# A decode attention kernel whose first V unit is split over two regions, with another layout for the transposed probabilities

## The chip, the cores and the metric

The kernel runs on one core of a Trainium2 chip. The metric is the device time of one execution in microseconds; the median of three runs before is 347.29 us.

## The reference

One decode step mixes two blocks with a gate. Attention has 2 batches, 32 heads, 4096 cached rows of 128, so K and V are 2 x 32 x 4096 x 128 bf16 each, 64 MB each: nearly all the data of the kernel.

```python
g = sigmoid((x * gate_w).sum(-1))                      # x: 2 x 1 x 512
q = (x @ wq) as (b, h, 1, 128)                         # 32 heads
p = softmax(einsum("bhqd,bhkd->bhqk", q, k_cache) * 128 ** -0.5)
a = einsum("bhqk,bhkd->bhqd", p, v_cache) as (b, 1, 4096) @ wo
b = maximum(x @ w1, 0) @ w2                            # 512 -> 1376 -> 512
out = g * a + (1 - g) * b
```

## The kernel before

**Units, halves and regions.** K and V are each cut into 8 units of 8 MB, unit u holding the rows of eight heads of one batch; each unit is laid over 128 partitions with 64 KB a partition. A half (`lo` or `hi`) is 4 MB. The buffer `kv` has five halves: region A (two), B (two), C (one). A piece is a unit in A or B, or a half in C (or in the first half of A or B). The lists `k_pieces` and `v_pieces` give the order by hand; `pieces` is K's ten, then V's ten. All pieces go out on SP's queue in that order (L279), and each waits for the marker `predecessor`: the last instruction that read the piece which held the same region (`holder`). Wait and issue are in order, so a piece that waits holds up all later ones. wq lies in C and w1 in B before K gets there; wo comes to C, and w2 to the upper half of B, after V.

**K.** Each half of a unit is four turns: VectorE transposes 128 x 2048 words in 32 x 32 blocks into one of three buffers `kt` (L393), and TensorE multiplies them with q (L400, L421), all scores staying in PSUM. The last transpose of a piece is its marker `k_read_n`.

**Softmax.** After the 64th turn VectorE takes the maximum (L429) and turns it about; ScalarE takes the four exponentials into `E_sb` (L441), laid out as [r, s] with 32 columns s for each r; VectorE transposes the 32 x 32 blocks in two instructions (L445) to `ET_sb`. `ET_sb` is [w, r]: for a fixed r, the 32 values of w that one block yields lie 64 elements (128 bytes) apart.

**V.** For each piece n, VectorE spreads the probabilities over a mask of eight groups (`v_spread`, L467) into `ptm`, one instruction for a piece (two for the first): 1024 elements a partition for a half, 2048 for a unit. Its source is read with neighbouring c 32 or 64 elements apart. TensorE multiplies them with the rows of V (`v_unit`, L482), 32 matmuls for a half and 64 for a unit, and the last is the marker `v_read_n`. VectorE takes the diagonal from PSUM (`v_extract`, L490, L493) into `X2`, five pieces to each batch. `v_spread` is called two pieces ahead, so on VectorE the spread of piece n + 2 stands in front of the extraction of piece n.

**End.** `o_gather` (L508 on) adds a batch's five pieces with f32 matmuls, scales them and turns them into `oW`; `project` (L527) multiplies by wo; `ffn_f` (L534) by w2 and adds; the output is stored.

Of the kernel before, what the change touches and what calls it, by code (L numbers as in the profile page):

```python
# [4 lines left out]
ALU = mybir.AluOpType  # L5
# [7 lines left out]

NKT = 3
HALF = 16384
REGION = {"A": 0, "B": 2 * HALF, "C": 4 * HALF}
WO_CUT = 24


# [68 lines left out]
def bass_gated_mix__gqa_block_cached__dense_activation_relu__decode_kernel(  # L88
# [39 lines left out]
    qbuf = sb("qbuf", [128, 4, 2, 4, 160], dt.bfloat16)  # L128
    kt_late = kt[:, :, :].rearrange("p k n -> p (k n)").bitcast(dt.bfloat16)
    E_sb = kt_late[:, 0:2048].rearrange("p (r s) -> p r s", s=32)  # L130
    ET_sb = kt_late[:, 2048:4096].rearrange("p (w r) -> p w r", r=64)
    ptm = kt_late[:, 4096:12288]
    q_late = qbuf[:].rearrange("p u a j m -> p (u a j m)").bitcast(dt.float32)
    X2 = q_late[:, 0:1280].rearrange("p (b k d) -> p b k d", b=2, d=128)
    pr_sb = q_late[:, 1280:1792]
    mpad = sb("mpad", [128, 32], dt.float32)
    mrow = sb("mrow", [128, 32], dt.float32)
    mmax = sb("mmax", [128, 8], dt.float32)
# [40 lines left out]
        P.sems[e] = nc.alloc_semaphore(e + "_ev")  # L179
    names = ["x", "gw", "wq", "w1", "wo0", "wo1", "w2a", "w2b", "w2c", "w2d", "out", "fin"]  # L180
    sem = {n: nc.alloc_semaphore("sem_" + n) for n in names}
    sem_region = {r: nc.alloc_semaphore("sem_region" + r) for r in "ABC"}

    mk = {}

    def marker(name):
        m = mk.get(name)
        if m is None:
            m = _Marker()
            mk[name] = m  # L190
        return m
# [2 lines left out]
    both, lo, hi = (0, 1), (0,), (1,)  # L194
    k_pieces = [(0, both, "A"), (1, both, "B"), (2, lo, "C"), (3, both, "A"), (4, both, "B"), (2, hi, "C"),
                (5, both, "A"), (6, both, "B"), (7, lo, "C"), (7, hi, "A")]
    v_pieces = [(0, both, "B"), (1, lo, "C"), (2, both, "A"), (3, both, "B"), (1, hi, "C"), (4, both, "A"),
                (5, both, "B"), (6, lo, "C"), (7, both, "A"), (6, hi, "B")]
    pieces = [("k", n, *p) for n, p in enumerate(k_pieces)] + [("v", n, *p) for n, p in enumerate(v_pieces)]
    landed, predecessor = {}, {}  # L200
    holder, filled = {"A": None, "B": "pe_h", "C": "pe_q"}, {"A": 0, "B": 0, "C": 0}
    for kind, n, u, halves, region in pieces:
        predecessor[kind, n] = holder[region]
        filled[region] += 1
        landed[kind, n] = (sem_region[region], 16 * filled[region])
        holder[region] = f"{kind}_read_{n}"

    turns = [(n, u, half, a, h, j == 0 and a == 0 and h == 0)
             for n, (u, halves, region) in enumerate(k_pieces) for j, half in enumerate(halves) for a in range(2) for h in range(2)]
# [60 lines left out]
    def sp(fn, waits=(), dwaits=()):  # L270
        P.add("sp", fn, waits=waits, dwaits=dwaits)
# [5 lines left out]
    for kind, n, u, halves, region in pieces:  # L277
        sp(lambda e, kind=kind, u=u, halves=halves, region=region:
           e.dma_start(piece_sb(halves, region), piece_in(kind, u, halves)).then_inc(sem_region[region], 16),  # L279
           waits=([marker(predecessor[kind, n])] if predecessor[kind, n] else []))  # L280
    sp(lambda e: e.dma_start(w2[0:96, 10, :], B_w2[1280:1376, :]).then_inc(sem["w2a"], 16), waits=[marker("v_read_6")])
    sp(lambda e: e.dma_start(wreg[:, 0:512 * WO_CUT], wo_in[:, 0:512 * WO_CUT]).then_inc(sem["wo0"], 16), waits=[marker("v_read_7")])
    sp(lambda e: e.dma_start(wreg[:, 512 * WO_CUT:HALF], wo_in[:, 512 * WO_CUT:HALF]).then_inc(sem["wo1"], 16))
    for name, r0, r1 in (("w2b", 0, 4), ("w2c", 4, 9), ("w2d", 9, 10)):
        sp(lambda e, name=name, r0=r0, r1=r1: e.dma_start(w2[:, r0:r1, :], w2a_in[:, r0:r1, :]).then_inc(sem[name], 16))
# [142 lines left out]
    def softmax():  # L428
        dve(lambda v: v.tensor_reduce(out=mpad[:, 0:2], in_=psf(0, 128, 0, 4 * BANK).rearrange("p (par n) -> p par n", par=2),  # L429
                                      axis=AX.X, op=ALU.max),  # L430
            waits=["pe_sc_63", "c_mpad"], signal="dve_m")
        dve(lambda v: v.transpose(out=mrow[:, :], in_=mpad[:, :]), waits=["dve_m"], signal="dve_mt")
        dve(lambda v: v.tensor_reduce(out=mmax[:], in_=mrow[:, :].rearrange("p (u c) -> p u c", c=4), axis=AX.X, op=ALU.max),
            waits=["dve_mt"], signal="dve_mm")
        dve(lambda v: v.tensor_scalar(out=nrow[:], in0=mmax[:].unsqueeze(2).to_broadcast([128, 8, 4]), scalar1=-INV_SQRT_DH,
                                      scalar2=None, op0=ALU.mult), waits=["dve_mm"], signal="dve_mn")
        dve(lambda v: v.transpose(out=negm[:, :], in_=nrow[:].rearrange("p u c -> p (u c)")),  # L437
            waits=["dve_mn"], signal="dve_neg")
        for g in range(2):
            for par in range(2):  # L440
                act(lambda a, g=g, par=par: a.activation(  # L441
                    out=E_sb[:, 32 * g:32 * g + 32, 16 * par:16 * par + 16], in_=psf(0, 128, (2 * par + g) * BANK, 512).rearrange("p (r s) -> p r s", s=16), func=ACT.Exp,
                    bias=negm[:, par:par + 1], scale=INV_SQRT_DH, accum_out=lsum[:, par, g:g + 1]),
                    waits=["dve_neg"], signal=f"act_exp{2 * g + par}")
            dve(lambda v, g=g: v.transpose(out=ET_sb[:, :, 32 * g:32 * g + 32].rearrange("p w r -> p r w"), in_=E_sb[:, 32 * g:32 * g + 32, :]),  # L445
                waits=[f"act_exp{2 * g + 1}"], signal=f"dve_et{g}")
        v_spread(0, 0, 32)
        v_spread(0, 32, 64)
        dve(lambda v: v.tensor_reduce(out=lrow[:], in_=lsum[:], axis=AX.X, op=ALU.add), waits=["act_exp3"], signal="dve_lrow")

    v_at, at = [], 0
# [5 lines left out]
        nh = len(v_pieces[n][1])  # L457
        return ptm[:, 1024 * v_at[n]:1024 * (v_at[n] + nh)].rearrange("p (n h c) -> p n h c", h=8, c=4)

    def v_spread(n, n0, n1):  # L460
        u, halves, region = v_pieces[n]
        nh = len(halves)
        w0 = 4 * u + 2 * halves[0]
        src = ET_sb[:, w0:w0 + 2 * nh, :].rearrange("p w r -> p (w r)").rearrange("p (c n) -> p n c", c=4)[:, n0:n1]
        used = {(v_at[n] + j) % 8 for j in range(nh)}
        prev = [m for m in range(n) if used & {v_at[m] + j for j in range(len(v_pieces[m][1]))}]
        dve(lambda v: v.tensor_tensor(out=v_weights(n)[:, n0:n1], in0=src.unsqueeze(2).to_broadcast([128, n1 - n0, 8, 4]),  # L467
                                      in1=mask8[:].unsqueeze(1).unsqueeze(3).to_broadcast([128, n1 - n0, 8, 4]), op=ALU.mult),
            waits=["dve_et1", "c_mask8"] + [f"v_read_{m}" for m in prev], signal=f"pt{n}_{n0}")

    def v_unit(n):
        u, halves, region = v_pieces[n]
        nn = 32 * len(halves)
        rows = piece_sb(halves, region).rearrange("p (c n d) -> p c n d", c=4, d=128)
        for j in range(nn):
            t = j % 4
            waits = []
            if j == 0:
                waits = [f"pt{n}_0"] + ([f"dve_m{n - 2}"] if n >= 2 else [])
            if n == 0 and j == 32:  # L480
                waits = ["pt0_32"]
            pe(lambda e, j=j, t=t: e.matmul(  # L482
                psf(32 * t, 32 * t + 32, V_BS[n % 2] * BANK, 512), lhsT=v_weights(n)[:, j],
                rhs=rows[:, :, j, :], start=(j < 4), stop=(j >= nn - 4), tile_position=(0, 32 * t)),
               waits=waits, dwaits=([landed["v", n]] if j == 0 else []), signal=(f"v_read_{n}" if j == nn - 1 else None))

    def v_extract(n):
        b, k = divmod(n, 5)
        parts = pr_sb.rearrange("p (c d) -> p c d", c=4)
        dve(lambda e: e.tensor_tensor(out=parts, in0=psf(0, 128, V_BS[n % 2] * BANK, 512).rearrange("p (c d) -> p c d", c=4),  # L490
                                      in1=maskc[:].unsqueeze(2).to_broadcast([128, 4, 128]), op=ALU.mult),
            waits=[f"v_read_{n}", "dve_maskc"] + ([f"dve_x{n - 1}"] if n else []), signal=f"dve_m{n}")
        dve(lambda e: e.tensor_reduce(out=X2[:, b, k, :], in_=parts.rearrange("p c d -> p d c"), axis=AX.X, op=ALU.add),  # L493
            waits=[f"dve_m{n}"], signal=f"dve_x{n}")
# [8 lines left out]
                signal=("dve_rinv" if b else None))  # L503

    def o_gather(b):
        for k in range(5):
            w0 = 24 - 8 * (v_pieces[5 * b + k][0] - 4 * b)
            pe(lambda e, k=k, w0=w0: e.matmul(psf(0, 32, O_C0, 128), lhsT=selx[:, w0:w0 + 32], rhs=X2[:, b, k, :],  # L508
                                              start=(k == 0), stop=(k == 4)),
               waits=[f"dve_x{5 * b + k}"] + (["dve_rinv", "dve_selx"] if k == 0 else []),  # L510
               signal=(f"pe_O{b}" if k == 4 else None))
        dve(lambda v, b=b: v.tensor_scalar(out=O_sb[:, b, :], in0=psf(0, 32, O_C0, 128), scalar1=rinv[:, b:b + 1],
                                           scalar2=gb[0:32, b:b + 1], op0=ALU.mult, op1=ALU.mult),
            waits=[f"pe_O{b}", "dve_rinv", "dve_g"], signal=f"dve_O{b}")
# [51 lines left out]
            k_scores(i - 1)  # L566
    k_scores(63)
    softmax()
    v_spread(1, 0, 32)
    for n in range(10):  # L570
        if n + 2 < 10:
            v_spread(n + 2, 0, 32 * len(v_pieces[n + 2][1]))
        v_unit(n)
        if n == 1:
            o_denominators()
        v_extract(n)
        if n == 5:
            o_gather(0)
    o_gather(1)
    project()  # L580
# [34 lines left out]
```

## Time and profile before

| | us |
|---|---|
| median of three runs | 347.29 (347.23 to 347.6) |
| the profiled execution's own time | 346.8 |
| its span, from first to last instruction | 345.3 |
| VectorE busy | 206.9 (60%) |
| TensorE busy | 198.2 (57%) |
| ScalarE busy | 14.8 (4%) |
| HBM read | 145.43 MB, 421 GB/s over the span |

Times in the profile count from the span's start. PE is TensorE's matmuls, PEld its weight loads, DVE VectorE, ACT ScalarE, SP the engine that issues the big transfers; L445 is line 445 of the kernel before. A group's row gives its count, then busy time and mean duration in ns, then the idle time ahead of it and what ended that. The chain that ended last is followed back from the last instruction. A transfer's time to landing counts from its issue, so it holds the time that it stood behind earlier ones.

### The profile page before, as it was taken

What the parts mean: (1) busy time and instruction counts of PE and PEld (TensorE: products, weight loads), DVE (VectorE), ACT (ScalarE), POOL (GpSimd) and SP (SyncE); (2) the same over time, 40 slices, a digit from 0 to 9 for tenths busy, and PEclk for the clock granted to TensorE, in tenths of its full rate; (3) what the DMA queues carried; (4) which work ended last, traced back from release to release, by engine and by line L of the source; (5) the groups of instructions that cost most, each with busy time, mean ns of one, the idle gap of its engine ahead of it and who ended that gap; (6) DMA issues with size and microseconds to landing.
All of it is one profiled execution on the core that took longest, in us unless ns stands there. A gap on an engine that the chain in (4) does not pass through costs nothing.

```text
span 345.3 us, 2491 instructions
## 1 busy us (share of the span) xinstructions
PE 198.2 (57%) x1230; PEld 54.0 (16%) x974; DVE 206.9 (60%) x129; ACT 14.8 (4%) x54; POOL 7.7 (2%) x20
## 2 busy tenths in 40 slices
PE   0430497997897996979999008150540523610655
PEld 0230021111111111211111003020210211200231
DVE  0400797996998996989998799741360060410131
ACT  1040001010001001000000300000000000000000
POOL 8000000000000000000000000000000000000000
PEclk9965599999899998998999757665785585665787
DMA  8998999989899999989989898999989899998995
GB/s 331 440 486 366 478 433 406 482 387 478 374 417 425 478 464 402 457 380 425 440 364 486 362 482 372 478 412 421 490 387 471 380 465 395 450 478 387 416 385 229
DMA packets 4019, 145.57 MB, mean 422 GB/s; under 512 B 453, under 2 KB 682, under 8 KB 938
## 3 DMA queue, kind: packets, MB, share of 16 engines
q1 hardware_dynamic: 4004, 145.43, 98.1%
q8 instruction: 8, 0.13, 0.1%
q14 instruction: 1, 0.01, 0.0%
q10 hardware_dynamic: 6, 0.00, 0.0%
HBM read 145.43 MB, written 0.00 MB: 421 GB/s over the span
## 4 chain that ended last, share of the span: by engine, by line
DMA 66%; DVE 19%; PE 13%; ACT 1%; issue 1%; SPq 0%; DVEq 0%
DMA kv<-in_A_k_cache_dram 28%; DMA kv<-in_A_v_cache_dram 24%; DVE kt L393 15%; DMA kv<-in_B_w_dram 11%; PE PS L482 4%; DMA kv<-in_A_wq_dram 4%; PE PS L421 3%; PE PS L400 3%; DVE kt L445 3%; PE PS L334 1%; PE PS L373 1%; DVE mpad L429 1%; DVE kt L467 1%; ACT qrow L347 0%; ACT kt L441 0%
## 5 line engine op out<-in xcount | busy, mean ns | idle before, releaser
L393 DVE STREAM_TRANSPOSE kt<-kv 128x2048 f32<-128x2048 f32 x64 | 141.1, 2273 | 24.5 <-DMA kv<-in_A_k_cache_dram 24.5
L421 PE MATMUL PS<-kt,qbuf 128*128 128x512 bf16 x256 | 106.3, 415 | 33.7 <-DVE kt L393 28.8
L400 PE MATMUL PS<-kt,qbuf 128*128 128x512 bf16 x256 | 105.7, 413 | 0.0
L482 PE MATMUL PS<-kv,kt 128*32 128x512 bf16 x512 | 46.9, 544 | 92.7 <-DMA kv<-in_A_v_cache_dram 76.7
L490 DVE TENSOR_TENSOR qbuf<-PS,maskc 128x512 f32<-128x512 f32 x10 | 6.9, 689 | 83.1 <-PE PS L482 83.0
L421 PEld LDWEIGHTS PS<-kt,qbuf 128*128 128x128 bf16 x256 | 25.6, 100 | 142.1 <-DVE kt L393 72.2
L482 PEld LDWEIGHTS PS<-kv,kt 128*32 128x32 bf16 x512 | 18.3, 129 | 120.3 <-issue 77.3
L467 DVE TENSOR_TENSOR kt<-kt,mask 128x1024 bf16<-128x1024 bf16 (+1 forms) x11 | 29.1, 2664 | 0.0
L329 ACT ACTIVATE qbuf<-PS 32x4 bf16<-32x4 bf16 (+1 forms) x40 | 7.6, 189 | 108.3 <-PE PS L400 106.9
L493 DVE TENSOR_REDUCE qbuf<-qbuf 128x128 f32<-128x512 f32 x10 | 10.2, 1019 | 0.3
L445 DVE STREAM_TRANSPOSE kt<-kt 128x1024 bf16<-128x1024 bf16 x2 | 9.3, 4825 | 1.5 <-ACT kt L441 1.5
L556 ACT ACTIVATE out_sb<-PS 2x128 bf16<-2x128 f32 x2 | 0.5, 270 | 146.9 <-PE PS L534 146.9
L334 PE MATMUL PS<-kv,xTw 128*32 128x512 bf16 x32 | 3.6, 631 | 3.2 <-DMA kv<-in_A_wq_dram 3.2
L441 ACT ACTIVATE kt<-PS,negm 128x512 bf16<-128x512 f32 x4 | 2.7, 684 | 58.8 <-DVE negm L437 58.8
L296 DVE COPY xT<-PS 128x12 bf16<-128x12 bf16 x1 | 0.2, 169 | 8.3 <-PE PS L293 8.3
L293 PE MATMUL PS<-ident,x_sb 3*128 3x3 bf16 x4 | 0.3, 166 | 8.0 <-DMA x_sb<-in_gate_w_dram 8.0
L350 DVE CAST qrow<-PS 128x256 bf16<-128x256 f32 x2 | 2.4, 1388 | 3.9 <-PE PS L334 3.9
L527 PE MATMUL PS<-kv,oW 128*2 128x512 bf16 x32 | 3.5, 618 | 1.8 <-DMA kv<-in_A_wo_dram 1.8
L232 POOL MEMSET qbuf<- 128x5120 bf16 x1 | 4.4, 4358 | 0.0
L508 PE MATMUL PS<-qbuf,selx 128*32 128x128 f32 x20 | 3.4, 325 | 0.3 <-DVE qbuf L493 0.3
L429 DVE TENSOR_REDUCE mpad<-PS 128x2 f32<-128x2048 f32 x1 | 2.3, 2292 | 2.2 <-PE PS L400 2.2
L530 DVE COPY qbuf<-PS 128x512 f32<-128x512 f32 x1 | 0.7, 692 | 4.5 <-PE PS L527 4.5
(62 smaller groups left out, 31.8 us busy)
## 6 DMA issues: line engine op xcount, KB each, us to landing
kv<-in_A_k_cache_dram SPq DMA_DIRECT2D x4, 4096.0 KB, 31.6
kv<-in_A_v_cache_dram SPq DMA_DIRECT2D x4, 4096.0 KB, 35.1
kv<-in_A_wq_dram SPq DMA_DIRECT2D x1, 4096.0 KB, 12.2
kv<-in_A_wo_dram SPq DMA_DIRECT2D x1, 3072.0 KB, 33.7
kv<-in_B_w_dram SPq DMA_DIRECT2D x1, 1376.0 KB, 15.0
kv<-in_A_wo_dram SPq DMA_DIRECT2D x1, 1024.0 KB, 35.8
kv<-in_B_w_dram SPq DMA_DIRECT2D x1, 640.0 KB, 37.7
kv<-in_B_w_dram SPq DMA_DIRECT2D x1, 512.0 KB, 36.6
```

What stands on the lines that cost most here:

```text
L232: pool(lambda g: g.memset(qbuf[:], 0.0), signal="c_qbuf")
L329: act(lambda a: a.activation(out=out, in_=src, func=ACT.Copy), waits=waits, signal=f"q_{b}_{u}_{blk}_{par}")
L334: pe(lambda e, n=n, t=t: e.matmul(psf(32 * (n % 4), 32 * (n % 4) + 32, (QR_B + n // 4) * BANK, 512), lhsT=xTw[:, t, :], rhs=wreg[:, t * 40 ...
L393: dve(lambda v: v.transpose(out=dst, in_=pairs[:, h, 64 * a:64 * a + 64, :]), waits=([f"pe_sc_{i - NKT}"] if i >= NKT else []), dwaits=([l ...
L400: return e.add_instruction(mybir.InstMatmult(start_tensor_calc=start, stop_tensor_calc=stop, tile_size=(128, 128), tile_position=(0, 0), l ...
L421: return e.matmul(out, lhsT=lhsT, rhs=rhs, start=start, stop=stop)
L429: dve(lambda v: v.tensor_reduce(out=mpad[:, 0:2], in_=psf(0, 128, 0, 4 * BANK).rearrange("p (par n) -> p par n", par=2), axis=AX.X, op=ALU ...
L445: dve(lambda v, g=g: v.transpose(out=ET_sb[:, :, 32 * g:32 * g + 32].rearrange("p w r -> p r w"), in_=E_sb[:, 32 * g:32 * g + 32, :]), wai ...
L467: dve(lambda v: v.tensor_tensor(out=v_weights(n)[:, n0:n1], in0=src.unsqueeze(2).to_broadcast([128, n1 - n0, 8, 4]), in1=mask8[:].unsqueez ...
L482: pe(lambda e, j=j, t=t: e.matmul(psf(32 * t, 32 * t + 32, V_BS[n % 2] * BANK, 512), lhsT=v_weights(n)[:, j], rhs=rows[:, :, j, :], start= ...
L490: dve(lambda e: e.tensor_tensor(out=parts, in0=psf(0, 128, V_BS[n % 2] * BANK, 512).rearrange("p (c d) -> p c d", c=4), in1=maskc[:].unsqu ...
L493: dve(lambda e: e.tensor_reduce(out=X2[:, b, k, :], in_=parts.rearrange("p c d -> p d c"), axis=AX.X, op=ALU.add), waits=[f"dve_m{n}"], si ...
```

## The change

Region A may now also be held as two halves, A and Ah. The V pieces become eleven: unit 0 as a half in Ah and a half in C, then the others, and unit 7 as two halves at the end, in A and Ah; unit 4 takes the place of unit 6 as the one that goes through C in halves. The first batch has five pieces, the second six. A piece waits for all the markers of what it overwrites. w2 and wo wait for the pieces that now hold B and C last.

`ET_sb` becomes [r, w]: the rows of a transposed block lie side by side, and each of the two transposes writes 1024 consecutive elements. The spread then reads neighbouring w: a unit is one instruction as before; a half is two instructions of 512 elements, one for each r2, each writing two of every four columns. The first spread is no longer cut into two by rows.

```diff
-REGION = {"A": 0, "B": 2 * HALF, "C": 4 * HALF}
+REGION = {"A": 0, "Ah": HALF, "B": 2 * HALF, "C": 4 * HALF}
...
-    ET_sb = kt_late[:, 2048:4096].rearrange("p (w r) -> p w r", r=64)
+    ET_sb = kt_late[:, 2048:4096].rearrange("p (r w) -> p r w", w=32)
...
-    v_pieces = [(0, both, "B"), (1, lo, "C"), (2, both, "A"), (3, both, "B"), (1, hi, "C"), (4, both, "A"),
-                (5, both, "B"), (6, lo, "C"), (7, both, "A"), (6, hi, "B")]
+    v_pieces = [(0, lo, "Ah"), (1, both, "B"), (0, hi, "C"), (2, both, "A"), (3, both, "B"), (4, lo, "C"), (5, both, "A"),
+                (6, both, "B"), (4, hi, "C"), (7, lo, "A"), (7, hi, "Ah")]
+    n_first = 5
...
     for kind, n, u, halves, region in pieces:
-        predecessor[kind, n] = holder[region]
+        parts = ["A", "Ah"] if region == "A" and len(halves) == 2 else [region]
+        predecessor[kind, n] = [m for r in parts for m in holder[r]]
...
-           waits=([marker(predecessor[kind, n])] if predecessor[kind, n] else []))
-    sp(lambda e: e.dma_start(w2[0:96, 10, :], B_w2[1280:1376, :]).then_inc(sem["w2a"], 16), waits=[marker("v_read_6")])
-    sp(lambda e: e.dma_start(wreg[:, 0:512 * WO_CUT], wo_in[:, 0:512 * WO_CUT]).then_inc(sem["wo0"], 16), waits=[marker("v_read_7")])
+           waits=[marker(m) for m in predecessor[kind, n]])
+    sp(lambda e: e.dma_start(w2[0:96, 10, :], B_w2[1280:1376, :]).then_inc(sem["w2a"], 16), waits=[marker(holder["B"][0])])
+    sp(lambda e: e.dma_start(wreg[:, 0:512 * WO_CUT], wo_in[:, 0:512 * WO_CUT]).then_inc(sem["wo0"], 16), waits=[marker(holder["C"][0])])
...
-            dve(lambda v, g=g: v.transpose(out=ET_sb[:, :, 32 * g:32 * g + 32].rearrange("p w r -> p r w"), in_=E_sb[:, 32 * g:32 * g + 32, :]),
+            dve(lambda v, g=g: v.transpose(out=kt_late[:, 2048 + 1024 * g:3072 + 1024 * g].rearrange("p (r w) -> p r w", w=32), in_=E_sb[:, 32 * g:32 * g + 32, :]),
                 waits=[f"act_exp{2 * g + 1}"], signal=f"dve_et{g}")
-        v_spread(0, 0, 32)
-        v_spread(0, 32, 64)
+        v_spread(0)
...
+        def spread(out, src, nc_, **kw):
+            shape = [128, src.shape[1], 8, nc_]
+            dve(lambda v: v.tensor_tensor(out=out, in0=src.unsqueeze(2).to_broadcast(shape),
+                                          in1=mask8[:].unsqueeze(1).unsqueeze(3).to_broadcast(shape), op=ALU.mult), waits=waits, **kw)
+
+        if len(halves) == 2:
+            spread(v_weights(n), ET_sb[:, :, w0:w0 + 4], 4, signal=f"pt{n}")
+        else:
+            for r2 in range(2):
+                spread(v_weights(n)[:, :, :, r2:4:2], ET_sb[:, 32 * r2:32 * r2 + 32, w0:w0 + 2], 2, signal=(f"pt{n}" if r2 else None))
...
     def o_gather(b):
-        for k in range(5):
+        mine = range(n_first) if b == 0 else range(n_first, len(v_pieces))
+        for n in mine:
```

More of the change, by code (lines that the diff above doesn't have):

```diff
@@ L130, in bass_gated_mix__gqa_block_cached__dense_activation_relu__decode_kernel @@
     E_sb = kt_late[:, 0:2048].rearrange("p (r s) -> p r s", s=32)
-    ET_sb = kt_late[:, 2048:4096].rearrange("p (w r) -> p w r", r=64)
+    ET_sb = kt_late[:, 2048:4096].rearrange("p (r w) -> p r w", w=32)
     ptm = kt_late[:, 4096:12288]
     q_late = qbuf[:].rearrange("p u a j m -> p (u a j m)").bitcast(dt.float32)
-    X2 = q_late[:, 0:1280].rearrange("p (b k d) -> p b k d", b=2, d=128)
-    pr_sb = q_late[:, 1280:1792]
+    X2 = q_late[:, 0:1536].rearrange("p (b k d) -> p b k d", b=2, d=128)
+    pr_sb = q_late[:, 1536:2048]
     mpad = sb("mpad", [128, 32], dt.float32)
@@ L181, in bass_gated_mix__gqa_block_cached__dense_activation_relu__decode_kernel @@
     sem = {n: nc.alloc_semaphore("sem_" + n) for n in names}
-    sem_region = {r: nc.alloc_semaphore("sem_region" + r) for r in "ABC"}
+    sem_region = {r: nc.alloc_semaphore("sem_region" + r) for r in REGION}
     mk = {}
@@ L196, in bass_gated_mix__gqa_block_cached__dense_activation_relu__decode_kernel @@
                 (5, both, "A"), (6, both, "B"), (7, lo, "C"), (7, hi, "A")]
-    v_pieces = [(0, both, "B"), (1, lo, "C"), (2, both, "A"), (3, both, "B"), (1, hi, "C"), (4, both, "A"),
-                (5, both, "B"), (6, lo, "C"), (7, both, "A"), (6, hi, "B")]
+    v_pieces = [(0, lo, "Ah"), (1, both, "B"), (0, hi, "C"), (2, both, "A"), (3, both, "B"), (4, lo, "C"), (5, both, "A"),
+                (6, both, "B"), (4, hi, "C"), (7, lo, "A"), (7, hi, "Ah")]
+    n_first = 5
     pieces = [("k", n, *p) for n, p in enumerate(k_pieces)] + [("v", n, *p) for n, p in enumerate(v_pieces)]
     landed, predecessor = {}, {}
-    holder, filled = {"A": None, "B": "pe_h", "C": "pe_q"}, {"A": 0, "B": 0, "C": 0}
+    holder = {"A": [], "Ah": [], "B": ["pe_h"], "C": ["pe_q"]}
+    filled = {r: 0 for r in REGION}
     for kind, n, u, halves, region in pieces:
-        predecessor[kind, n] = holder[region]
+        parts = ["A", "Ah"] if region == "A" and len(halves) == 2 else [region]
+        predecessor[kind, n] = [m for r in parts for m in holder[r]]
         filled[region] += 1
         landed[kind, n] = (sem_region[region], 16 * filled[region])
-        holder[region] = f"{kind}_read_{n}"
+        for r in parts:
+            holder[r] = [f"{kind}_read_{n}"]
     turns = [(n, u, half, a, h, j == 0 and a == 0 and h == 0)
@@ L458, in v_weights, with v_spread @@
         return ptm[:, 1024 * v_at[n]:1024 * (v_at[n] + nh)].rearrange("p (n h c) -> p n h c", h=8, c=4)
-    def v_spread(n, n0, n1):
+    def v_spread(n):
         u, halves, region = v_pieces[n]
-        nh = len(halves)
         w0 = 4 * u + 2 * halves[0]
-        src = ET_sb[:, w0:w0 + 2 * nh, :].rearrange("p w r -> p (w r)").rearrange("p (c n) -> p n c", c=4)[:, n0:n1]
-        used = {(v_at[n] + j) % 8 for j in range(nh)}
+        used = {(v_at[n] + j) % 8 for j in range(len(halves))}
         prev = [m for m in range(n) if used & {v_at[m] + j for j in range(len(v_pieces[m][1]))}]
-        dve(lambda v: v.tensor_tensor(out=v_weights(n)[:, n0:n1], in0=src.unsqueeze(2).to_broadcast([128, n1 - n0, 8, 4]),
-                                      in1=mask8[:].unsqueeze(1).unsqueeze(3).to_broadcast([128, n1 - n0, 8, 4]), op=ALU.mult),
-            waits=["dve_et1", "c_mask8"] + [f"v_read_{m}" for m in prev], signal=f"pt{n}_{n0}")
+        waits = ["dve_et1", "c_mask8"] + [f"v_read_{m}" for m in prev]
+        def spread(out, src, nc_, **kw):
[7 more added lines that the diff above has]
+                spread(v_weights(n)[:, :, :, r2:4:2], ET_sb[:, 32 * r2:32 * r2 + 32, w0:w0 + 2], 2, signal=(f"pt{n}" if r2 else None))
     def v_unit(n):
@@ L478, in v_unit @@
             if j == 0:
-                waits = [f"pt{n}_0"] + ([f"dve_m{n - 2}"] if n >= 2 else [])
-            if n == 0 and j == 32:
-                waits = ["pt0_32"]
+                waits = [f"pt{n}"] + ([f"dve_m{n - 2}"] if n >= 2 else [])
             pe(lambda e, j=j, t=t: e.matmul(
@@ L487, in v_extract @@
     def v_extract(n):
-        b, k = divmod(n, 5)
+        b, k = divmod(n, n_first) if n < n_first else (1, n - n_first)
         parts = pr_sb.rearrange("p (c d) -> p c d", c=4)
@@ L505, in o_gather @@
     def o_gather(b):
-        for k in range(5):
[L507 to L511, printed above, removed]
+        mine = range(n_first) if b == 0 else range(n_first, len(v_pieces))
+        for n in mine:
+            w0 = 24 - 8 * (v_pieces[n][0] - 4 * b)
+            pe(lambda e, n=n, w0=w0: e.matmul(psf(0, 32, O_C0, 128), lhsT=selx[:, w0:w0 + 32], rhs=X2[:, b, n - mine[0], :],
+                                              start=(n == mine[0]), stop=(n == mine[-1])),
+               waits=[f"dve_x{n}"] + (["dve_rinv", "dve_selx"] if n == mine[0] else []),
+               signal=(f"pe_O{b}" if n == mine[-1] else None))
         dve(lambda v, b=b: v.tensor_scalar(out=O_sb[:, b, :], in0=psf(0, 32, O_C0, 128), scalar1=rinv[:, b:b + 1],
@@ L568, in bass_gated_mix__gqa_block_cached__dense_activation_relu__decode_kernel @@
     softmax()
[L569 to L572, printed above, removed]
+    v_spread(1)
+    for n in range(len(v_pieces)):
+        if n + 2 < len(v_pieces):
+            v_spread(n + 2)
         v_unit(n)
@@ L576, in bass_gated_mix__gqa_block_cached__dense_activation_relu__decode_kernel @@
         v_extract(n)
-        if n == 5:
+        if n == n_first:
             o_gather(0)
```

## The prediction

> **What bounds the kernel now.** I read the page first: the span, the slices, the queues and the chain.
>
> ```profile
> span 345.3 us, 2491 instructions
> ...
> DMA  8998999989899999989989898999989899998995
> ...
> q1 hardware_dynamic: 4004, 145.43, 98.1%
> ...
> DMA 66%; DVE 19%; PE 13%; ACT 1%; issue 1%; SPq 0%; DVEq 0%
> ```
>
> One queue, SP's, moves 145 MB, and its packets fill 98.1% of sixteen engines' span. Two thirds of the chain that ended last is transfers. No engine edit can be worth anything unless it keeps this queue from running dry, and the most that it can be worth is the time in which the queue was dry. So the second view is the stretches (columns: stretch, length, busy time of PE, PEld, DVE, ACT and POOL, the granted TensorE clock, the DMA share, GB/s).
>
> ```profile
> 60.00:160.00 100.00, 86.83 (x329) 16.42 (x164) 91.38 (x43) 4.28 (x24) 0.00 (x0) 0.95 1.01 435
> 170.00:171.00 1.00, 0.86 (x5) 0.10 (x2) 1.00 (x2) 0.00 (x0) 0.00 (x0) 1.00 0.31 131
> 171.00:172.00 1.00, 1.00 (x5) 0.25 (x3) 1.00 (x1) 0.00 (x0) 0.00 (x0) 1.00 0.77 262
> 165.00:225.00 60.00, 34.20 (x216) 8.65 (x171) 53.87 (x31) 2.78 (x8) 0.00 (x0) 0.80 0.99 422
> ```
>
> A hundred microseconds of K run at 435 GB/s. At 170 to 172, where the last K piece is out and the first V piece begins, the rate falls to 131 and 262. Over 165 to 225 the mean is 422: 60 x 13/435 = 1.8 us of bytes are missing.
>
> The third view, issues on SP's queue in order of time, with (fourth view) the time from each issue to its landing, says why and how much.
>
> ```profile
> 151.57 0.33 SPq L279 DMA_DIRECT2D kv<-in_A_k_cache_dram  x1
> 170.93 0.33 SPq L279 DMA_DIRECT2D kv<-in_A_v_cache_dram  x1
> 188.47 0.33 SPq L279 DMA_DIRECT2D kv<-in_A_v_cache_dram  x1
> 212.57 0.33 SPq L279 DMA_DIRECT2D kv<-in_A_v_cache_dram  x1
> 214.30 0.33 SPq L279 DMA_DIRECT2D kv<-in_A_v_cache_dram  x1
> 229.31 0.33 SPq L279 DMA_DIRECT2D kv<-in_A_v_cache_dram  x1
> ```
>
> ```profile
> kv<-in_A_k_cache_dram SPq DMA_DIRECT2D x1, 4096.0 KB, 21.0
> kv<-in_A_v_cache_dram SPq DMA_DIRECT2D x1, 21.8
> kv<-in_A_v_cache_dram SPq DMA_DIRECT2D x1, 34.4
> kv<-in_A_v_cache_dram SPq DMA_DIRECT2D x1, 29.7
> kv<-in_A_v_cache_dram SPq DMA_DIRECT2D x1, 4096.0 KB, 37.7
> kv<-in_A_v_cache_dram SPq DMA_DIRECT2D x1, 42.0
> ```
>
> The rows of the two fences pair in order (the second V piece, a half into C, is left out): the last K half lands at 151.57 + 21.0 = 172.57, the first V unit at 192.7, the third V piece (region A) at 222.87, the fourth (B) at 242.27, the fifth (C) at 252.0, the sixth (A again) at 271.31. From 172.57 to 222.87 the queue moves 8 + 4 + 8 MB in 50.30 us; from 222.87 to 271.31 again 8 + 4 + 8 MB, in 48.44. The difference, **1.86 us**, is the hole; it agrees with the 1.8 above. Five halves in 48.44 us make **9.69 us per 4 MB half** when the queue is full. The cause is the second issue: the unit into region B goes out at 170.93, when VectorE has read the K unit there, only 1.64 us before the transfer ahead of it lands. The third issue is far ahead of need, and after it no hole comes: the rate is back for good.
>
> **The early half.** Piece V0 becomes the low half of unit 0 in Ah, the upper half of region A. Ah is free when K unit 5 has been read, which is what the K half issued at 151.57 waits for too; so V0 goes out right behind it, near 152. At 170.93 the queue then holds 1.64 + 9.69 us of work in place of 1.64. The hole goes: **-1.86 us** (1.6 to 2.1 by what lies between the two readings and their rounding). Bytes are the same.
>
> **What is late next.** V0, V1 (unit 1 in B, issued 170.93) and V2 (the other half of unit 0 in C, issued near 180) now end at 172.57 + 4 x 9.69 = 211.3. The next, V3 (unit 2 in A), overwrites Ah and so waits for TensorE's reading of V0; all later issues stand behind it on SP. Before, the piece that waited for the first V reading was issued at 212.57 with work queued until 222.87, a lead of 10.3 us. What lead does an issue need? A lead of 1.64 us cost 1.86, so 3.5 us should be free and each microsecond less costs one: the due time is 211.3 - 3.5 = 207.8. When does TensorE end with V0? Rows of the stretch between scores and V (group rows: busy, mean ns; then the timeline: start, length):
>
> ```profile
> L445 DVE STREAM_TRANSPOSE kt<-kt 128x1024 bf16<-128x1024 bf16 x2 | 9.3, 4825 | 1.5 <-ACT kt L441 1.5
> L432 DVE STREAM_TRANSPOSE mrow<-mpad 128x32 f32<-128x32 f32 x1 | 0.2, 211 | 0.0
> ```
>
> ```profile
> L393 DVE STREAM_TRANSPOSE kt<-kv 128x2048 f32<-128x2048 f32 x64 | 141.1, 2273 | 24.5 <-DMA kv<-in_A_k_cache_dram 24.5
> ```
>
> ```profile
> L467 DVE TENSOR_TENSOR kt<-kt,mask 128x2048 bf16<-128x2048 bf16 x4 | 14.3, 3579 | 0.0
> L467 DVE TENSOR_TENSOR kt<-kt,mask 128x1024 bf16<-128x1024 bf16 x3 | 5.6, 1851 | 0.0
> ```
>
> ```profile
> 196.42 0.21 ACT L441 ACTIVATION_READ_ACCUMULATOR kt<-PS,negm 128x1 f32 x1
> 195.33 9.28 DVE L445 STREAM_TRANSPOSE kt<-kt 128x1024 bf16<-128x1024 bf16 x2 [1.51 <-ACT kt L441]
> 206.57 7.68 PE L482 MATMUL PS<-kv,kt 128*32 128x512 bf16 x96 [16.01 <-DVE kt L467]
> 252.14 3.53 PE L482 MATMUL PS<-kv,kt 128*32 128x512 bf16 x32 [4.61 <-DMA kv<-in_A_v_cache_dram]
> ```
>
> *Transposes.* Each takes 4825 ns now, 4.7 ns per element, and writes its elements 128 bytes apart. In the new layout a block's row is 32 neighbouring elements, as at L393. L393 and L432 give (2273 - 211)/(2048 - 32) = 1.02 ns per element, so 1024 elements take 211 + 992 x 1.02 = 1.23 us. That is the lower end, 4.83 (no change) the upper. I take 1.23, since L393 has the same kind of write; its type is another, which leaves the doubt. The first runs 195.33 to 196.56, the second from 196.66 (the last exponential's accumulator is read at 196.63) to 197.9.
>
> The trace of before cannot part two causes, the spread-out writes and the two-byte type. The Trainium skill, "SBUF — State Buffer", section Door 1, says that SBUF has 16-byte lines and that each access crossing into a new line pays a penalty: by that rule the new writes lose their cost and the sum stays at 345.4; were it the type, it would be the 347.7 of the first rival. No trace here shows it yet.
>
> *Spreads.* A half is now two instructions of 512 elements, where it was one of 1024. The slope of the two L467 forms is (3579 - 1851)/1024 = 1.69 ns, so 512 take 1851 - 864 = 0.99 us, and two 1.97. The reads are now in runs of two or four where they were 64 or 128 bytes apart (1.02 ns per element at best: 0.6 each); the writes skip every second element (4.7 at worst: 2.4 each). I take 1.97, the instruction's own row: V0's weights are ready at 199.9. *Matmuls.* A half took 3.53 us (252.14). TensorE ends with V0 at **203.4**, 4.4 us before the due time of 207.8; V3 goes out with no hole. In before, by the same sum with the old transposes, it would be 195.33 + 9.28 + 1.97 + 3.53 = 210.1. So the new layout of the transposes is what pays for the early half: alone it would be worth nothing, as in the old order the lead there is 10.3 us already.
>
> *Later pieces.* V4 waits for V1's reading: V1 lands at 201.6, its 128x2048 spread ends at 199.9 + 0.2 + 3.6 = 203.7, 64 matmuls make it about 210, against a queue that lasts until 211.3 + 19.4 = 230.7. All later issues lead by 15 us or more; the last V half then lands at 172.57 + 16 x 9.69 = 327.6. The second half of w2's 96 rows and wo are now issued behind V7 and V8 (about 305 and 312) in place of 297.69 and 303.88, still 15 us before the queue would be dry. These, the eleven issues in place of ten (0.33 us each on SP, far ahead) and the longer VectorE list (two 512s for each half) cost nothing under that cover.
>
> **The tail.** The last V piece is a half in both kernels, with the same transfers behind it.
>
> ```profile
> 303.88 0.34 SPq L282 DMA_DIRECT2D kv<-in_A_wo_dram  x1
> 332.66 1.78 PE L508 MATMUL PS<-qbuf,selx 128*32 128x128 f32 x8
> 335.96 0.20 DVE L519 CAST oW<-PS 128x32 bf16<-128x32 f32 x1 [0.36 <-PE PS L516]
> 337.70 3.51 PE L527 MATMUL PS<-kv,oW 128*2 128x512 bf16 x32 [1.78 <-DMA kv<-in_A_wo_dram]
> ```
>
> ```profile
> kv<-in_A_wo_dram SPq DMA_DIRECT2D x1, 3072.0 KB, 33.7
> ```
>
> The projection waits for wo (303.88 + 33.7 = 337.58), not for the cast that ended at 336.16: 1.4 us of slack. The second batch gathers six pieces in place of five, two more f32 passes of 1.78/8 = 0.22 us: 0.4 us at most, covered. Everything from wo's landing on moves with the queue.
>
> **The sum.** -1.86 + 0 + 0: span 345.3 to 343.4, the profiled execution 346.8 to 344.9. Against the median of the three runs, 347.29: **345.4 us** (-0.54%). About 0.2%, 0.7 us, is what a measurement of this kernel can tell from no change.
>
> **Rivals.**
> *Same: the transposes stay at 4.8 us.* Then V0 is read at 210.1, 2.3 us after the due time: the hole moves from 172 to 211 and is 2.3 in place of 1.86. 347.29 + 0.4 = 347.7. For it: the type differs from L393's. Against it: the gap of 4.7 to 1.02 ns per element is large for a type, and the old writes are far apart. Chance 0.10.
> *Same: each further transfer costs a fixed time.* The Trainium skill, "DMA: Bandwidth & Descriptors", section Anatomy of one DMA, fits about 2.0 us plus bytes at 436 GB/s to one DMA (of the other kind of queue); by it the eleventh V transfer gives back the whole gain. As a mechanism here: a fixed cost per transfer would show as a half that takes more than half a unit's time. After 222.87 the unit lands 19.40 us on and the half another 9.73: half a unit's 9.70 and 0.03 over. To give no change one more transfer would have to cost the whole 1.86 us, 347.3. Chance 0.04.
> *Slower: the first reading comes too late by far.* One mechanism, V3's wait on V0's reading: from 207.8 each microsecond costs one, past 209.7 the kernel is slower than before. It needs the old transposes and the strided spread writes at the old transposes' rate too (2.4 us each): 195.33 + 9.28 + 4.8 + 3.53 = 212.9, a hole of 5.1 us, 347.29 - 1.86 + 5.1 = 350.5. With fast transposes even such spreads end at 206.2, in time. Chance 0.06.
>
> **How the numbers follow.** Forecast 0.80, the two that give no change 0.14, slower 0.06; so faster 0.80, same 0.14, slower 0.06. The forecast's own range is 347.23 - 2.1 to 347.6 - 1.6, that is 345.1 to 346.0, with a little below for a run's spread: 344.9. To leave out no more than 2 in 10 the range goes up over the case of the old transposes: 344.9 to 347.8.
>
> **What would show it.** Right: in the changed profile the V issue right behind the one near 151.6; no slice near 170 to 172 under 400 GB/s; landings 9.69 us per half across the border, so V2 at about 211.3; transposes near 1.2 us, TensorE's first V matmul near 200, V3 issued near 203.5; span near 343.4. Wrong: V3's issue after 208 and a fall of the rate near 211; a half that takes over 9.9 us between landings; or a projection that waits for the cast and not for wo.

## The result and the profile after

The changed kernel takes 345.23 us (median of six, 345.01 to 345.3) against 347.3 us (347.12 to 347.6) before: a ratio of 0.9938, 95% interval 0.9926 to 0.9951: a small gain, but clear of noise. The span goes from 345.3 to 343.5 us, the profiled execution from 346.8 to 345.01. Forecast were 345.4, 343.4 and 344.9.

The stretches of the changed kernel (columns as in the prediction):

```profile
60.00:160.00 100.00, 86.53 (x332) 16.30 (x165) 91.29 (x43) 4.28 (x24) 0.00 (x0) 0.97 1.01 434
170.00:171.00 1.00, 0.91 (x4) 0.10 (x1) 1.00 (x2) 0.00 (x0) 0.00 (x0) 1.00 1.23 524
171.00:172.00 1.00, 0.96 (x5) 0.29 (x3) 1.00 (x1) 0.00 (x0) 0.00 (x0) 1.00 1.06 459
165.00:225.00 60.00, 35.80 (x227) 9.12 (x178) 45.07 (x36) 2.79 (x8) 0.00 (x0) 0.81 1.01 434
```

At 170 to 172 stood 131 and 262 GB/s; now the rate runs through, and 165 to 225 has K's own 434 where it had 422. (A transfer moves in packets, and a packet counts in the slice in which it starts, so the rate of one short slice swings; the landings below are the firmer sign.) The issues on SP's queue, with the times to landing in the same order:

```profile
152.02 0.43 SPq L283 DMA_DIRECT2D kv<-in_A_v_cache_dram  x1
171.01 0.33 SPq L283 DMA_DIRECT2D kv<-in_A_v_cache_dram  x1
179.78 0.33 SPq L283 DMA_DIRECT2D kv<-in_A_v_cache_dram  x1
203.13 0.33 SPq L283 DMA_DIRECT2D kv<-in_A_v_cache_dram  x1
```

```profile
kv<-in_A_v_cache_dram SPq DMA_DIRECT2D x1, 4096.0 KB, 30.3
kv<-in_A_v_cache_dram SPq DMA_DIRECT2D x1, 30.7
kv<-in_A_v_cache_dram SPq DMA_DIRECT2D x1, 4096.0 KB, 31.7
kv<-in_A_v_cache_dram SPq DMA_DIRECT2D x1, 27.7
```

V0, the first V piece, goes out right behind the last K half and lands at 182.3, V1 at 201.7, V2 at 211.5, V3 at 230.8: 9.7 us to the half across the whole border. V3 is issued at 203.13, far ahead of 211.5, because VectorE, and so TensorE's reading of V0, is done so early (timeline of VectorE, then of TensorE; then two group rows):

```profile
195.41 2.58 DVE L449 STREAM_TRANSPOSE kt<-kt 128x1024 bf16<-128x1024 bf16 x2 [1.52 <-ACT kt L445]
198.03 1.33 DVE L472 TENSOR_TENSOR kt<-kt,mask 128x512 bf16<-128x512 bf16 x2
199.42 8.27 PE L490 MATMUL PS<-kv,kt 128*32 128x512 bf16 x96 [8.78 <-DVE lrow L452]
```

```profile
L449 DVE STREAM_TRANSPOSE kt<-kt 128x1024 bf16<-128x1024 bf16 x2 | 2.5, 1245 | 1.6 <-ACT kt L445 1.5
L472 DVE TENSOR_TENSOR kt<-kt,mask 128x2048 bf16<-128x2048 bf16 x3 | 6.8, 2280 | 0.0
```

The transposes take 1245 ns where they took 4825, the spread of a unit 2280 where it took 3579.

### The profile page after: what moved, and what is told of

Same layout as the page of the kernel before. It is cut to its first block, busy times and chain, and to the rows that moved or that the text cites. A ratio compares the mean times of both kernels' runs of the same rounds, so it can differ in the third digit from the quotient of the medians.

```text
span 343.5 us, 2507 instructions
## 1 busy us (share of the span) xinstructions
PE 198.0 (58%) x1232; PEld 54.0 (16%) x976; DVE 192.2 (56%) x137; ACT 14.8 (4%) x54; POOL 7.7 (2%) x20
## 4 chain that ended last, share of the span: by engine, by line
DMA 75%; DVE 16%; PE 7%; issue 1%; ACT 0%; SPq 0%; DVEq 0%
DMA kv<-in_A_v_cache_dram 35%; DMA kv<-in_A_k_cache_dram 28%; DVE kt L397 16%; DMA kv<-in_B_w_dram 8%; DMA kv<-in_A_wq_dram 4%; PE PS L490 3%; PE PS L425 1%; PE PS L404 1%; PE PS L338 1%; PE PS L377 1%; ACT qrow L351 0%; PE PS L357 0%; PE PS L543 0%; DVE out_sb L563 0%; SPq L287 0%
## 5 line engine op out<-in xcount | busy, mean ns | idle before, releaser
L490 PE MATMUL PS<-kv,kt 128*32 128x512 bf16 x512 | 48.7, 560 | 89.7 <-DMA kv<-in_A_v_cache_dram 80.9
L498 DVE TENSOR_TENSOR qbuf<-PS,maskc 128x512 f32<-128x512 f32 x11 | 7.6, 691 | 95.5 <-PE PS L490 95.5
L472 DVE TENSOR_TENSOR kt<-kt,mask 128x512 bf16<-128x512 bf16 (+1 forms) x17 | 19.3, 1181 | 0.0
L501 DVE TENSOR_REDUCE qbuf<-qbuf 128x128 f32<-128x512 f32 x11 | 11.2, 1021 | 0.4
L449 DVE STREAM_TRANSPOSE kt<-kt 128x1024 bf16<-128x1024 bf16 x2 | 2.5, 1245 | 1.6 <-ACT kt L445 1.5
L536 PE MATMUL PS<-kv,oW 128*2 128x512 bf16 x32 | 2.1, 378 | 2.0 <-DMA kv<-in_A_wo_dram 2.0
```

The lines of the kernel that those rows point to most:

```text
L472: dve(lambda v: v.tensor_tensor(out=out, in0=src.unsqueeze(2).to_broadcast(shape), in1=mask8[:].unsqueeze(1).unsqueeze(3).to_broadcast(sha ...
L490: pe(lambda e, j=j, t=t: e.matmul(psf(32 * t, 32 * t + 32, V_BS[n % 2] * BANK, 512), lhsT=v_weights(n)[:, j], rhs=rows[:, :, j, :], start= ...
```

## The experiments

Theory: all of the gain is the hole in SP's queue between K and V; the order of pieces closes it, the layout of the probabilities only brings V3's issue in time. The rivals are that the order alone, or VectorE's shorter work alone, is the gain. Each ratio is against the kernel before, run beside the variant (medians 347.22 to 347.45 us); rows and landings come from one profiled execution of each kernel.

**The two parts one by one.** The new order with the transposes and spreads of before:

```diff
-    ET_sb = kt_late[:, 2048:4096].rearrange("p (r w) -> p r w", w=32)
+    ET_sb = kt_late[:, 2048:4096].rearrange("p (w r) -> p w r", r=64)
...
-            spread(v_weights(n), ET_sb[:, :, w0:w0 + 4], 4, signal=f"pt{n}")
...
+        src = ET_sb[:, w0:w0 + 2 * nh, :].rearrange("p w r -> p (w r)").rearrange("p (c n) -> p n c", c=4)
```

> The changed kernel with its new order of V pieces, but with the transposes and spreads of before (probabilities as [w, r], one spread instruction of 1024 elements for a half). Theory (the refill hangs on the first V reading, which the layout makes early enough): the transposes take 2 x 4.8 us again, the first piece is read near 210.1, V3 is issued near 210.2, 1.3 us before the transfers ahead of it land at 211.4; by 3.5 minus the lead a hole of 2.2 us opens near 211, and the time is 345.2 + 2.2 = 347.4 us, no change against before. Rival (the early half alone brings the gain, the layout is idle time): 345.2 us, no hole near 211.

Measured: 348.08 us, ratio 1.0023 (1.0013 to 1.0033): 0.2% slower than before, and 2.85 us over the changed kernel. Its stretches, then (timeline) its transposes and the issue of V3:

```profile
170.00:171.00 1.00, 0.92 (x4) 0.10 (x1) 1.00 (x2) 0.00 (x0) 0.00 (x0) 1.00 1.15 492
208.00:209.00 1.00, 1.00 (x16) 0.40 (x12) 1.00 (x1) 0.00 (x0) 0.00 (x0) 0.50 0.68 295
209.00:210.00 1.00, 1.00 (x12) 0.16 (x4) 1.00 (x1) 0.00 (x0) 0.00 (x0) 0.50 0.31 131
210.00:211.00 1.00, 0.87 (x16) 0.34 (x16) 1.00 (x2) 0.00 (x0) 0.00 (x0) 0.96 0.00 0
213.00:214.00 1.00, 1.00 (x21) 0.36 (x14) 1.00 (x2) 0.00 (x0) 0.00 (x0) 1.00 0.00 0
```

```profile
195.43 9.29 DVE L449 STREAM_TRANSPOSE kt<-kt 128x1024 bf16<-128x1024 bf16 x2 [1.51 <-ACT kt L445]
210.35 0.33 SPq L283 DMA_DIRECT2D kv<-in_A_v_cache_dram  x1
```

The hole at 170 is gone and another stands near 210, where for a microsecond no packet starts. A slice with 0 GB/s alone does not prove a hole: 213 to 214 shows 0 as well, and there the queue is full again. The landings do prove it: the first of the sixteen DMA engines is done with all that was issued at 209.51, and V3 goes out only at 210.35. Place and cause are the theory's; its size is 0.7 us over the expected.

The old order with the new layout:

```diff
-    ET_sb = kt_late[:, 2048:4096].rearrange("p (w r) -> p w r", r=64)
+    ET_sb = kt_late[:, 2048:4096].rearrange("p (r w) -> p r w", w=32)
...
-            dve(lambda v, g=g: v.transpose(out=ET_sb[:, :, 32 * g:32 * g + 32].rearrange("p w r -> p r w"), in_=E_sb[:, 32 * g:32 * g + 32, :]),
+            dve(lambda v, g=g: v.transpose(out=kt_late[:, 2048 + 1024 * g:3072 + 1024 * g].rearrange("p (r w) -> p r w", w=32), in_=E_sb[:, 32 * g:32 * g + 32, :]),
...
+            spread(v_weights(n), ET_sb[:, :, w0:w0 + 4], 4, signal=f"pt{n}")
```

> The kernel before with the new layout of the probabilities alone (transposes and spreads of the changed kernel, order of V pieces as before). Theory: the first V piece is read some 6 us earlier, where the lead was 10.3 us already; the hole at 171 stays; 347.3 us, within 0.2% of before. Rival (less VectorE work on the path is the gain): the 7 us saved in the transposes would show in part, 345.2 us or less.

Measured: 347.19 us, ratio 0.9998 (0.999 to 1.0007). Its stretch at the border and its transposes:

```profile
170.00:171.00 1.00, 0.87 (x5) 0.10 (x2) 1.00 (x2) 0.00 (x0) 0.00 (x0) 1.00 0.31 131
```

```profile
195.34 2.58 DVE L445 STREAM_TRANSPOSE kt<-kt 128x1024 bf16<-128x1024 bf16 x2 [1.51 <-ACT kt L441]
```

The transposes are 6.7 us shorter, the hole stays, the time stays. This order alone costs 0.9 us, the layout alone is worth nothing; the two together are worth 2.07 us.

**How late may V3's issue be?** The changed kernel with idle reductions in front of the first spread; the edit shows two, the other runs have `(4, 4, 2)` and `(4, 4, 4, 4)` in the loop:

```diff
+    idle = sb("idle", [128, 8], dt.float32)
...
+        for k, nb in enumerate((4, 4)):
+            dve(lambda v, k=k, nb=nb: v.tensor_reduce(out=idle[:, k:k + 1], in_=psf(0, 128, 0, nb * BANK).unsqueeze(1), axis=AX.X, op=ALU.max),
+                waits=["act_exp3"])
         v_spread(0)
```

> The changed kernel with two idle reductions over PSUM (2.29 us each, their results unused) on VectorE between the transposes and the first spread: the first V piece is read 4.6 us later, V3 is issued near 207.7, 3.7 us before the transfers ahead of it land at 211.4. Theory (an issue needs a lead of 3.5 us, and each microsecond less costs one): no hole, 345.2 us. Rival (any later reading costs its own time, the VectorE chain is on the path): 345.2 + 4.6 = 349.8 us.

> The same with two whole and one half idle reduction (5.8 us): V3 issued near 208.9, a lead of 2.5 us. Theory: a hole of 1.0 us, 346.2 us. A due time of 1.6 us or less of lead would give 345.2; the VectorE chain on the path 351.0.

> The same with four idle reductions (9.2 us): V3 issued near 212.3, 0.9 us after the last landing ahead of it. Theory: a hole of 3.5 + 0.9 = 4.4 us near 212, 349.6 us. The VectorE chain on the path: 354.4 us.

Measured: 345.41 us (0.9949, 0.9934 to 0.9965), 346.32 us (0.9973, 0.9964 to 0.9982), 349.39 us (1.0058, 1.0046 to 1.007). The two reductions of the first, then V3's issue in the three, in this order, then the stretch of the hole in the third:

```profile
198.14 4.45 DVE L453 TENSOR_REDUCE idle<-PS 128x1 f32<-128x2048 f32 x2
```

```profile
207.24 6.82 SPq L284 DMA_DIRECT2D kv<-in_A_v_cache_dram  x3
```

```profile
208.27 5.88 SPq L284 DMA_DIRECT2D kv<-in_A_v_cache_dram  x3
```

```profile
211.72 0.33 SPq L284 DMA_DIRECT2D kv<-in_A_v_cache_dram  x1
```

```profile
210.00:211.00 1.00, 1.00 (x16) 0.35 (x12) 1.00 (x3) 0.00 (x0) 0.00 (x0) 0.50 0.00 0
211.00:212.00 1.00, 1.00 (x16) 0.43 (x12) 0.83 (x2) 0.00 (x0) 0.00 (x0) 0.50 0.00 0
```

(The first two rows of SP's queue merge V3's issue, at the time that they give, with the two after it.) 4.45 us more of VectorE time in the chain cost next to nothing: 0.2 us between the medians, though the six runs spread from 345.11 to 346.93. Beyond that it is paid for. The expected times fit to 0.2 us, in part by luck: the issues came about 0.5 us earlier than expected. By the lead that was measured, 211.59 - 208.27 = 3.3 us, the rule of 3.5 gives 0.2 us for the second run, and its time shows 1.1.

The rule is better told by engines. The landing events in the traces count the sixteen DMA engines one by one. With F for the landing on the first engine to be done with V2 (the last K half, for the kernel before), and the delay for how much later than 19.34 us (the changed kernel's figure) after F the first engine lands the unit behind it:

| kernel | issue | F | issue - F | delay | delay - (issue - F) |
|---|---|---|---|---|---|
| changed | 203.13 | 209.41 | -6.28 | 0 | |
| two reductions | 207.24 | 209.53 | -2.29 | 0.19 | |
| two and a half | 208.27 | 209.57 | -1.30 | 0.52 | 1.82 |
| before (at 171) | 170.93 | 170.82 | 0.11 | 1.96 | 1.85 |
| new order, old layout | 210.35 | 209.51 | 0.84 | 2.71 | 1.87 |
| four reductions | 211.72 | 209.44 | 2.28 | 4.18 | 1.90 |

In this queue an issue is free if it comes some 1.9 us before the first engine runs dry, and from there the first landing behind it is later one for one, at either place. The median times follow the delay to 0.2 us (2.07 us for the hole before, 2.85 and 4.16 over the changed kernel for the last two rows), except in the run with two and a half reductions: 1.1 us of time for 0.52 of delay. There one engine is 2.46 us behind the first from the unit after V3 on, where the changed kernel has 2.03; no run settles why.

**Does the layout matter in any other way?** The old transposes and spreads once more, in an order in which no issue depends on the first reading until much later:

```diff
-    v_pieces = [(0, lo, "Ah"), (1, both, "B"), (0, hi, "C"), (2, both, "A"), (3, both, "B"), (4, lo, "C"), (5, both, "A"),
-                (6, both, "B"), (4, hi, "C"), (7, lo, "A"), (7, hi, "Ah")]
-    n_first = 5
+    v_pieces = [(0, lo, "Ah"), (1, both, "B"), (0, hi, "C"), (2, lo, "A"), (2, hi, "Ah"), (3, both, "B"), (4, lo, "C"),
+                (5, both, "A"), (6, both, "B"), (4, hi, "C"), (7, both, "A")]
+    n_first = 6
...
```

> The old transposes and spreads again, but an order of V pieces in which the refill does not hang on the first reading: unit 0 as halves in Ah and C, unit 1 in B, then unit 2 as two halves, its low half into A (which waits for the last K transpose near 188.5 alone) and its high half into Ah (which waits for the reading of the first piece near 210); unit 7 whole at the end. The low half of unit 2 covers 9.7 us more, so the issue near 210 comes 9 us or so before the first engine would run dry near 219. Theory (a hole opens only when an issue comes later than about 1.9 us before the first engine has drained; the layout matters through that alone): no hole, 345.2 us, 0.6% under the kernel before. Rival (the slow transposes cost time on the path by themselves): 347.4 us or more, as with the new order and the old layout.

Measured: 345.14 us, ratio 0.9938 (0.9924 to 0.9951), the changed kernel's own. Rows of its SP queue, of its transposes and of the stretch where the old layout had its hole:

```profile
188.71 0.33 SPq L283 DMA_DIRECT2D kv<-in_A_v_cache_dram  x1
210.46 0.33 SPq L283 DMA_DIRECT2D kv<-in_A_v_cache_dram  x1
195.57 9.29 DVE L449 STREAM_TRANSPOSE kt<-kt 128x1024 bf16<-128x1024 bf16 x2 [1.51 <-ACT kt L445]
```

```profile
210.00:211.00 1.00, 0.92 (x16) 0.25 (x16) 1.00 (x2) 0.00 (x0) 0.00 (x0) 0.69 0.91 393
```

The transposes take their 9.29 us and V's first reading sends its issue out at 210.46, as late as with the new order and the old layout (210.35); but the half issued at 188.71 covers it, and the whole gain is there. So the layout is worth just the lead of one issue. (Unit 7 is whole in this order; the run under "The end" shows that this changes nothing.)

**Transfers.** The changed kernel with each unit as two transfers:

```diff
-        filled[region] += 1
+        filled[region] += len(halves)
...
-        sp(lambda e, kind=kind, u=u, halves=halves, region=region:
-           e.dma_start(piece_sb(halves, region), piece_in(kind, u, halves)).then_inc(sem_region[region], 16),
-           waits=[marker(m) for m in predecessor[kind, n]])
+        for k, half in enumerate(halves):
+            sp(lambda e, kind=kind, u=u, half=half, k=k, region=region:
+               e.dma_start(kv[:, REGION[region] + HALF * k:REGION[region] + HALF * (k + 1)], piece_in(kind, u, (half,))).then_inc(sem_region[region], 16),
+               waits=[marker(m) for m in predecessor[kind, n]])
```

> The changed kernel with each 8 MB unit of K and V issued as two 4 MB transfers, one behind the other, to the same place: eleven more transfers. Theory (in a queue that never runs dry a transfer has no fixed cost to speak of, at most 0.03 to 0.1 us): 345.2 to 346.3 us. Rival (a fixed cost of about 2 us to each transfer): 11 x 2 = 22 us more, 367 us; a rival with the fixed cost partly hidden would be anywhere above 346.5.

Measured: 345.8 us, ratio 0.9962 (0.9949 to 0.9974); span 344.2 against 343.5. Eleven more transfers cost 0.6 to 0.8 us, 0.05 to 0.07 us each. The Trainium skill, "DMA: Bandwidth & Descriptors", section Anatomy of one DMA, fits about 2.0 us fixed to each DMA, of another kind of queue. In this queue, which always holds another transfer, no more than 0.07 us of it shows; whether the rest is hidden or is not there on this kind of queue, no run tells.

**The end.** The changed kernel with unit 7 whole:

```diff
-                (6, both, "B"), (4, hi, "C"), (7, lo, "A"), (7, hi, "Ah")]
+                (6, both, "B"), (4, hi, "C"), (7, both, "A")]
```

> The changed kernel with unit 7 as one piece in A at the end, in place of two halves. The queue moves the same bytes in the same order. Theory: TensorE can start on unit 7 only when all of it has landed near 328.1, so 64 matmuls (6.5 us) stand there in place of 32 (3.6 us); the cast of oW ends near 337.7 in place of 335.0, past the landing of wo near 335.7, the projection's 32 matmuls (3.5 us) end near 341.3 and the last matmuls near 343.1 in place of 341.6: 345.2 + 1.4 = 346.6 us. Rival (the end hangs on the last transfers alone, so the last halves are worth nothing): 345.2 us.

Measured: 344.81 us, ratio 0.9937 (0.9924 to 0.9951): the same as with two halves. The expectation missed by 1.8 us, and the rival held: the end hangs on the last transfers. The end in timeline and stretch, then the stretch of the projection in the kernel before:

```profile
328.34 5.54 PE L490 MATMUL PS<-kv,kt 128*32 128x512 bf16 x64 [16.26 <-DMA kv<-in_A_v_cache_dram]
336.92 0.19 DVE L528 CAST oW<-PS 128x32 bf16<-128x32 f32 x1 [0.35 <-PE PS L525]
337.76 1.90 PE L536 MATMUL PS<-kv,oW 128*2 128x512 bf16 x32 [0.88 <-DVE PS L532]
341.15 0.55 PE L543 MATMUL PS<-kv,hT 128*2 128x128 bf16 x24 [0.29 <-DMA kv<-in_B_w_dram]
```

```profile
337.70:339.60 1.90, 1.84 (x40) 0.79 (x44) 0.01 (x1) 0.00 (x0) 0.00 (x0) 1.00 0.93 372
```

```profile
337.00:341.00 4.00, 3.30 (x32) 1.05 (x36) 0.00 (x0) 0.00 (x0) 0.00 (x0) 0.57 1.00 404
```

The cast does come after wo, at 337.1, as expected. But the projection's 32 matmuls then run without a pause at a granted clock of 1.00 and take 1.90 us; I had taken 3.51 from the kernel before, where the clock was 0.57. They are done at 339.7, and the last matmuls wait for w2's transfer (341.15) as ever. So splitting the last unit buys nothing here.

## Why the prediction was right

- *The hole at the border, -1.86 us.* Right: it is gone; the medians differ by 2.07 us, the spans by 1.8. That the rates gave 1.8 beside the 1.86 of the landings was in part luck: packets count where they start, and the same stretch ended at 224 in place of 225 has a mean of 428 GB/s, which makes 0.9 us. The landings carry the term.
- *TensorE done with V0 at 203.4, against a due time of 207.8.* Right: V3 is issued at 203.13. The weights were ready 0.5 us earlier than in the sum and the reading took 0.2 us longer, so two small errors partly cancel. The due time holds: 207.24 is all but free, 208.27 costs 1.1 us of time (0.5 past the due time), 211.72 4.2 us (3.9 past it). That the layout alone would be worth nothing was right; the part of the sum beside it, "the new layout of the transposes is what pays for the early half", was right for this order and, as the last order shows, is not the only way to pay.
- *The terms.* Transposes 1.23 us each forecast, 1.245 measured: the type is the same, so the cost was the spread-out writes. The Trainium skill's 16-byte lines ("SBUF — State Buffer", section Door 1) point the right way here; no run parts lines from any other cost of distance. Two spreads of a half were put at 1.97 us and took 1.33: reading neighbours paid there too, and 2280 ns for 2048 elements is 1.1 ns each. This error lay under the cover of 4.4 us and cost nothing.
- *The lead rule.* The lead of 3.5 us before the last landing came from one hole, at which the engines landed 1.75 us apart. Near 211 they land 2.03 us apart in the changed kernel, 1.91 with the old layout, so the rule is better counted from the first engine. The first rival's hole was put at 2.3 us and measured 2.71 at the first engine, 2.85 in the time: about 0.2 of that is the spread of the engines, 0.25 an issue that came later than the sum had it (210.35 for 210.1). The rival's place was right, its total of 347.7 should have been 348.1, on the slower side.
- *The tail.* Covered, as forecast, but with 0.7 us left and not the 1.0 of the sum (1.4 less 0.4): the last V half took 3.59 us, at a granted clock of 0.50, where the kernel before had 2.91, at 0.63. wo's landing still starts the projection:

```profile
334.83 0.20 DVE L528 CAST oW<-PS 128x32 bf16<-128x32 f32 x1 [0.35 <-PE PS L525]
335.85 1.47 PE L536 MATMUL PS<-kv,oW 128*2 128x512 bf16 x24 [1.06 <-DMA kv<-in_A_wo_dram]
```

- *The fixed cost of a transfer* (a rival that the rows put at 0.03 us for one more): right to dismiss it, 0.05 to 0.07.

## What to carry to other kernels

When one DMA queue is busy 98% of the span, look for the stretch where its rate falls, and read from the issue just ahead of it which wait let it run dry. Here 6.7 us less of VectorE work bought nothing by itself. Closing one such hole moves the question to the next issue whose lead has shrunk, so list the leads of all later issues before and after; an engine that was idle time before may become what sets the lead. A lead can be won by a faster engine or by a piece order in which the issue depends on something older, and both were worth the same here (345.23 and 345.14 us).

## What the runs showed that I had not expected

The sixteen DMA engines do not stay together. In the changed kernel fifteen land the first K unit within 0.52 us and the sixteenth 1.94 us after the first; by the last V piece but one, eight of them are 1.5 to 2.0 us late. The trace has eight transfers of 16 KB of the kind "instruction", and after each of the first ones (27.8, 93.1, 143.7 us) one more engine is late by about 1.45 us; another, late by 0.95 us, follows one of 8 KB at 122.2. That they are the cause fits in time; no run took one away. After a hole the engines are together again (0.57 us apart at 192 in the kernel before, 0.51 at 232 in the new order with the old layout), so a hole hides part of this lateness until the next fetch: in the latter the unit V3 lands 1.3 us later than in the changed kernel on the last engine, the unit behind it 2.8 us.
